# Linformer attention and a maxout layer on one core: first up blocks in two parts by heads, a split load, and a load moved

## The chip, the cores and the metric

The kernel runs on one core of a Trainium2 chip. The core has TensorE (matrix products; in profiles PE, its weight loads PEld), VectorE (DVE), ScalarE (ACT), GpSimd (POOL) and SyncE (SP), which here only issues transfers. Sixteen DMA engines move data between HBM and on-chip memory. The metric is the device time of one execution in microseconds, lower is better.

## What is computed

```python
k_proj = einsum('ks,bhsd->bhkd', E, k);  v_proj = einsum('ks,bhsd->bhkd', F, v)
attn = softmax(q @ k_proj^T / sqrt(64))           # over 64 projected keys
x = (attn @ v_proj) as rows (batch, position), columns (head, feature)
out = maximum(x @ w1, x @ w2) @ w_out
```

Batch 8, 8 heads, sequence 1024, head size 64, 64 projected keys; x is 8192 x 512, w1 and w2 are 512 x 1024, w_out is 1024 x 512. Inputs and output are float32.

## The kernel before

Loads go through GpSimd's queue and turn float32 into float16 on the way. The order of work on each engine is written out by hand: `manual_schedule` keeps the program's order, and each engine runs its own instructions in that order, with semaphores between the engines.

The maxout is rewritten: `max(h1, h2) = relu(x (w1 - w2)) + x w2`, so that `out = relu(x wd) w_out + x m`, with `wd = w1 - w2` (`step_wd`, L418, VectorE, 256 columns at a time) and `m = w2 w_out` (`step_w2t`, transposes L427 and a copy L433; `step_m`, L440 with the cast L444). An "up" is a product with wd and the relu, a "down" is the product with w_out and m together. Batch 0's ups are plain (`up_slots`: 8 blocks `fb` of 128 rows for each half `j` of the positions, each block a sum of four products L404 over r, the chunks of 128 columns of x; relu on ScalarE, L411, for the first three blocks and on VectorE, L413, for the others). Chunks r = 0, 1 are heads 0 to 3, chunks 2, 3 are heads 4 to 7. All later ups (`up_steps`, L558) and all downs (`down_steps`, L636) use a scheme with seven products instead of eight and sums on VectorE (L519 inputs, L475 weights, L573 and L660 outputs).

A batch's attention consists of: `step_kv` (L180, projections of k and v; casts L191, L193, L196), `step_kpt` (transposes of the projected k, L211, copy L216), `step_qt` (transposes of q, L237, copy L242), `step_sc` (scores, L266, exponential L306), `step_dn` (sums L278, logarithm L312), `step_inv` (exponential of minus the logarithm, L316), `step_at` (values L278, product with the inverse sums L329 into `xt`). Each of these works on a group (g: 4 heads, j: half the positions). From batch 2 on, q (L249), and from batch 3 on also the projected k (L223), are transposed by DMA transposes that SP issues, and `step_group` does scores (L266) of one group beside sums and values of the one before.

Batch 0's attention comes first and alone, with "warming" products `warm` (L140) where TensorE would wait. Then `slots`, the hand-made list: batch 0's up blocks, interleaved with step_wd and step_w2t, then the four step_m, then the units (a unit is half a batch; unit n's down pieces interleaved with unit n+1's ups). `steps` hangs further work behind named slots: `("P", n, p, i)` is piece i of product p of unit n's down, `("U", n, h, i)` an up product, `("G", n, h)` a mark for a group of scores. Batch 1's attention is hung behind step_m and the pieces of unit 0's down by the list of strings that begins `"kv", "", "kpt", "qt00 qt10"`.

On-chip memory for k, v and q has four buffers for all batches (`kvq`); the next load waits until one is free. `loads(b, ...)` issues a batch's loads. `step_gate` (L229) is a one-element copy on GpSimd that reads a transposed tile, so that loads behind it on that queue wait until the DMA transpose has landed. Accumulators lie in eight banks: four single ones (mm0 to mm3), which `mm_bank()` hands out in rotation, or by number, and two pairs (`att_banks`). After step_m the rotation is cut to mm2 and mm3, and downs use mm0 and mm1 by number.

```python
def mm_bank(dtype=FP32, n=None):
    if n is None:
        n = turn.pop(0)
        turn.append(n)
    return ps.tile([128, 512 if dtype == FP32 else 1024], dtype, tag=f"mm{n}", name="mm_ps")
```

Of the kernel before, what the change touches and what calls it, by code (L numbers as in the profile page):

```python
# [12 lines left out]
ALU = mybir.AluOpType  # L13
# [3 lines left out]
def kernel(  # L17
# [12 lines left out]
    nc = tc.nc  # L30
# [14 lines left out]
    const = ctx.enter_context(tc.tile_pool(name="const", bufs=1))  # L45
    kvq = ctx.enter_context(tc.tile_pool(name="kvq", bufs=4))
    proj = ctx.enter_context(tc.tile_pool(name="proj", bufs=2))
    soft = ctx.enter_context(tc.tile_pool(name="soft", bufs=3))
    qtp = ctx.enter_context(tc.tile_pool(name="qtp", bufs=2))
    stage = ctx.enter_context(tc.tile_pool(name="stage", bufs=4))  # L50
    xpool = ctx.enter_context(tc.tile_pool(name="xpool", bufs=3))
    gpool = ctx.enter_context(tc.tile_pool(name="gpool", bufs=2))
    opool = ctx.enter_context(tc.tile_pool(name="opool", bufs=4))
    ppool = ctx.enter_context(tc.tile_pool(name="ppool", bufs=4))
# [5 lines left out]
# [6 lines that stand above are left out]
    def att_banks(dtype=FP32):  # L66
        return ps.tile(
            [128, 2, 512 if dtype == FP32 else 1024], dtype, tag="att", bufs=2, name="att_ps"
        )
# [50 lines left out]
    w1_sb = big(1).rearrange("p (r f) -> p r f", r=NDC)  # L120
    w2_sb = big(2).rearrange("p (r f) -> p r f", r=NDC)
    wo_sb = const.tile([128, NFB, DM], FP16)
    for f0, f1 in ((0, 256), (256, 512), (512, DF)):
        for w_sb, w in ((w2_sb, moe_w2), (w1_sb, moe_w1)):
            for z in range(2):
                nc.gpsimd.dma_start(
                    out=w_sb.rearrange("p (g z) f -> p g z f", z=2)[:, :, z, f0:f1],
                    in_=w.rearrange("(g p z) f -> p g z f", p=128, z=2)[:, :, z, f0:f1],
                )
# [4 lines left out]
    junk = const.tile([1, 1], FP16)  # L134


    def warm(n):
        w_ps = mm_bank()
        for _ in range(n):
            nc.tensor.matmul(  # L140
                out=w_ps, lhsT=ones16[:, 0:128], rhs=ones16, start=True, stop=True
            )
# [29 lines left out]
    def step_kv(t, h0=0, h1=H, which="kv", att=False, dma=False):  # L172
        kv_ps = att_banks()[:, 0, :] if att else mm_bank()
        n = (h1 - h0) * D
        both = which == "v"
        for c in range(NC):
            for w in which:
                i = "kv".index(w)
                for r in range(2) if both else (i,):
                    nc.tensor.matmul(  # L180
                        out=kv_ps[r * KP : (r + 1) * KP, 0:n],
                        lhsT=eft[:, i, c, :],
                        rhs=t[w][:, h0:h1, c, :],
                        start=(c == 0), stop=(c == NC - 1),
                    )
        fl = lambda ap: ap[:, h0:h1].rearrange("p h z d -> p (h z d)")
        zd = lambda ap: ap.rearrange("p (h d z) -> p h z d", d=D // 2, z=2)
        if "k" in which:
            eng = nc.vector.tensor_copy if which == "k" else nc.scalar.copy
            kp = t["kp"][:, h0:h1]  # L190
            eng(out=kp[:, :, 0, :], in_=kv_ps[0:KP, 0:n].rearrange("p (h d) -> p h d", d=D))  # L191
        if both:
            nc.vector.tensor_copy(out=t["vp"][:, h0:h1], in_=zd(kv_ps[:, 0:n]))  # L193
        elif "v" in which:
            def finish_v():
                nc.vector.tensor_copy(out=t["vp"][KP:128, h0:h1], in_=zd(kv_ps[KP:128, 0:n]))  # L196
                if dma:
                    nc.vector.tensor_copy(out=kp[:, :, 1, :], in_=kp[:, :, 0, :])
                    step_kpt_dma(t)
                nc.vector.tensor_copy(out=fl(t["vp"][0:KP]), in_=fl(t["vp"][KP:128]))  # L200

            if att:
                return finish_v
            finish_v()
# [109 lines left out]
    def step_inv(t, g, j):  # L314
        ld = t["ld", g, j]
        nc.scalar.activation(out=ld, in_=ld, func=ACTF.Exp, scale=-1.0)  # L316

    def step_at(t, g, j, att=False):
        if "xt" not in t:
            new_xt(t)  # L320
        ld = t.pop(("ld", g, j))
        if att:
            both = att_banks()
            at_ps = [both[:, o, :] for o in range(2)]
        else:
            at_ps = [mm_bank() for _ in range(2)]
        values_into(t, g, j, at_ps)
        for o in range(2):
            nc.vector.tensor_tensor(  # L329
                out=x_out(t, g, j)[:, :, o, :],  # L330
                in0=at_ps[o].rearrange("q (z n) -> q z n", z=2),
                in1=ld[:, o, None, :].broadcast_to([128, 2, W]),
                op=ALU.mult,
            )
# [63 lines left out]
    def up_slots(t, j):  # L398
        t["gt", j] = gt = gpool.tile([128, NFB, HALF], FP16, tag="gt", name="gt_sb")
        for fb in range(NFB):  # L400
            def up(fb=fb):
                h_ps = mm_bank()
                for r in range(NDC):
                    nc.tensor.matmul(  # L404
                        out=h_ps,
                        lhsT=wd_sb[:, r, fb * 128 : (fb + 1) * 128],
                        rhs=t["xt"][:, r, :, j * W : (j + 1) * W],
                        start=(r == 0), stop=(r == NDC - 1),
                    )
                if fb < 3:  # L410
                    nc.scalar.activation(out=gt[:, fb, :], in_=h_ps, func=ACTF.Relu)  # L411
                else:
                    nc.vector.tensor_scalar_max(gt[:, fb, :], h_ps, 0.0)  # L413
            yield up


    def step_wd(f0):
        nc.vector.tensor_tensor(  # L418
            out=wd_sb[:, :, f0 : f0 + 256], in0=w1_sb[:, :, f0 : f0 + 256],
            in1=w2_sb[:, :, f0 : f0 + 256], op=ALU.subtract,  # L420
        )

    def step_w2t(f0):
# [309 lines left out]
    step_kpt(t, 4, 8)  # L733
    step_dn(t, 0, 1)
    step_inv(t, 0, 0)
    warm(4)
    step_qt(t, 4, 4, 0, NI // 2)
    step_qt(t, 4, 4, NI // 2, NI)
# [2 lines left out]
    step_sc(t, 1, 1)  # L741
    step_kv(t, 0, 4, "v")
    step_dn(t, 1, 0)
    step_inv(t, 1, 0)
    step_at(t, 0, 0)
    step_dn(t, 1, 1)
    step_inv(t, 0, 1)
    step_kv(t, 4, 8, "v")
    step_inv(t, 1, 1)
    step_at(t, 1, 0)  # L750
    step_wd(0)
    step_at(t, 0, 1, True)
    step_at(t, 1, 1, True)
    warm(4)


    load_all(tiles[1], 1, "k", k)
    u0, u1 = [*up_slots(t, 0)], [*up_slots(t, 1)]
    wt = [lambda f0=f0: step_w2t(f0) for f0 in range(0, DF, 256)]
    wd = [lambda f0=f0: step_wd(f0) for f0 in range(0, DF, 256)]  # L760
    f = lambda s, *a: lambda: s(tiles[0], *a)

    def loads(b, *names):
        for n in names:
            b_ = b + (n == "k" and b < 2)
            if b_ < B:
                load_all(tiles[b_], b_, n, {"k": k, "v": v, "q": q}[n])

    slots = [
        (0, u0[0]), (1, u0[1]), (None, lambda: loads(1, "v", "q", "k")), (2, u1[0]), (3, u1[1]),  # L770
        (None, wd[1]), (4, u0[2]), (None, wt[0]), (5, u0[3]),
        (None, wd[2]), (None, wt[1]), (6, u1[2]), (7, u1[3]), (8, u0[4]), (9, u0[5]), (None, wd[3]),
        (None, wt[2]), (10, u1[4]), (11, u1[5]), (12, u0[6]), (13, u0[7]), (None, wt[3]),
        (14, u1[6]), (15, u1[7]),
        *((16 + n, lambda n=n: step_m(n)) for n in range(NDC)),
    ]
# [26 lines left out]
    def at_slot(key, s, *a):  # L803
        steps.setdefault(key, []).append(lambda: s(*a))
# [12 lines left out]
    at_slot((0, 19), new_attn, t)  # L817
    at_slot((0, 19), lambda: turn.__setitem__(slice(None), [2, 3]))
    for n, x in enumerate((
        "kv", "", "kpt", "qt00 qt10", "", "sc00 sc10", "qt01", "qt11", "",  # L820
        "dn00 in00 dn10 in10", "", "", "at00 AT10 sc01", "", "",
    )):
        key = ("P", 0, (n - 1) // 2, (n - 1) % 2) if n else (0, 19)
        for name in x.split():
            if name[0] == "k":
                if name == "kpt":
                    at_slot(key, step_kpt, t, 0, H, True)
                else:
                    at_slot(key, step_kv, t, 0, H, "kv", True)
                    at_slot(key, loads, 2, "v", "q")  # L830
            else:
                g, j = int(name[2]), int(name[3])
                s_ = {"qt": step_qt, "sc": step_sc,
                      "dn": step_dn, "in": step_inv, "at": step_at, "AT": step_at}[name[:2]]
                args = (4 * g, 4, 2 * j, 2 * j + 2) if name[:2] == "qt" else (g, j)
                at_slot(key, s_, t, *args, *([True] if name[:2] == "AT" else []))
        if n in (1, 5):
            at_slot(key, step_t, 1, (0, 1) if n == 1 else (2, 3))
        if 6 <= n < 10:
            at_slot(key, sums_x, U[0, 1], ((2, 0, 1, 3)[n - 6],))  # L840
# [6 lines left out]
    at_slot(("G", 1, 0), step_qt_dma, t, 0, H // 2)  # L847
    at_slot(("G", 1, 0), step_qt_dma, t, H // 2, H)
    at_slot(("U", 1, 0, 6), step_gate, t, "qt")
    at_slot(("U", 1, 0, 6), loads, 3, "k", "v", "q")  # L850

    for b in range(3, B):
        t = tiles[b]
# [75 lines left out]
```

## Time and profile before

| | |
|---|---|
| median of 7 runs | 328.0 us (327.59 to 329.59) |
| the profiled execution's own time | 327.64 us |
| its span | 325.9 us |
| TensorE clock granted | full in all slices |
| loads issued by GpSimd (q0) | 28.31 MB, 54.7% of the 16 engines' span |
| stores, DMA transposes (q1) | 24.25 MB, 31.1% |
| k of batch 1, of batch 2 (1 MB each): issue to landing | 16.4 us, 29.0 us |

The span is the time from the first to the last instruction in the record. Columns of the timeline are start, duration, engine, line, operation, what it writes and reads, shape and count, then in brackets the idle time before it and what ended it. In a list of issues the last number is the time from issue to landing. In a table of windows the busy time and count of each engine stand in the order PE, PEld, DVE, ACT, POOL, then the TensorE clock, the DMA share and GB/s. Durations of products are given to the end of their pipeline; one behind another, a 128x512 product takes 0.216 us of TensorE.

### The profile page before, as it was taken

The numbers are of one execution on the slowest core, as the hardware profiler recorded it, in microseconds if no ns is written. First come the engines' busy times: TensorE is split into PE (matmuls) and PEld (weight loads), VectorE is DVE, ScalarE is ACT, GpSimd is POOL, SyncE is SP. The second block draws the span as 40 slices with busy tenths as digits, with TensorE's granted clock in tenths as the row PEclk, the third lists the DMA queues.
The fourth block names the chain that finished last, engine by engine and source line by source line (L and its number), as shares of the span: only waits on it lengthen the run. The fifth ranks groups of instructions, "written<-read, shape, count | busy, mean of one in ns | idle before, by whom it ended". The sixth has DMA issues, their size and how long they took to land.

```text
span 325.9 us, 9015 instructions
## 1 busy us (share of the span) xinstructions
PE 317.1 (97%) x3856; PEld 248.7 (76%) x3856; DVE 239.5 (74%) x424; ACT 201.1 (62%) x359; POOL 37.0 (11%) x56
## 2 busy tenths in 40 slices
PE   8989999999999999999999999999999999999994
PEld 4554547877887788878887888878887888888883
DVE  1355898985969788777967796977967796969572
ACT  2465322566776677667776777657776777765541
POOL 8646002003000200003000300003000000000000
PEclk9999999999999999999999999999999999999999
DMA  8999999987999799996999699989999120212032
GB/s 157 205 200 199 207 208 207 218 203 141 200 235 227 105 166 241 201 183 97 219 209 180 110 183 239 198 164 126 229 197 213 31 100 32 99 34 99 33 131 97
DMA packets 74680, 53.14 MB, mean 163 GB/s; under 512 B 29456, under 2 KB 74512, under 8 KB 74640
## 3 DMA queue, kind: packets, MB, share of 16 engines
q0 software_dynamic: 29376, 28.31, 54.7%
q1 hardware_dynamic: 45264, 24.25, 31.1%
q8 instruction: 30, 0.49, 0.6%
q14 instruction: 10, 0.08, 0.1%
HBM read 57.15 MB, written 16.78 MB: 227 GB/s over the span
## 4 chain that ended last, share of the span: by engine, by line
PE 87%; DMA 5%; DVE 3%; POOL 2%; issue 1%; ACT 0%; DVEq 0%; POOLq 0%
PE mm_ps L636 44%; PE mm_ps L558 26%; PE att_ps L180 4%; DMA v_sb<-in_v_dram 4%; PE mm_ps L404 4%; PE att_ps L278 3%; PE mm_ps L266 3%; PE mm_ps L440 2%; DMA big<-in_moe_w_dram 2%; POOL q_sb L102 1%; POOL k_sb L102 1%; DVE gt_sb L573 1%; DVE o_sb L660 1%; PE mm_ps L427 1%; PE mm_ps L237 0%
## 5 line engine op out<-in xcount | busy, mean ns | idle before, releaser
L529 ACT COPY p_sb<-mm_ps 128x512 f32<-128x512 f32 x172 | 97.1, 594 | 43.0 <-PE mm_ps L558 30.7
L636 PEld LDWEIGHTS <-big 128*128 128x128 f16 x768 | 73.6, 98 | 12.0 <-issue 3.5
L636 PE MATMUL mm_ps<-T_sb,big 128*128 128x256 f16 x576 | 77.9, 273 | 0.0
L573 DVE TENSOR_TENSOR gt_sb<-mm_ps,p_sb 128x512 f16<-128x512 f32 x56 | 38.5, 688 | 45.8 <-PE mm_ps L558 42.6
L558 PE MATMUL mm_ps<-big,big 128*128 128x256 f16 x336 | 50.4, 273 | 0.0
L558 PEld LDWEIGHTS <-big 128*128 128x128 f16 x448 | 43.8, 98 | 5.3 <-issue 0.2
L636 PEld LDWEIGHTS <-gt_sb 128*128 128x128 f16 x384 | 35.7, 98 | 9.7 <-issue 5.4
L636 PE MATMUL mm_ps<-wo_sb,gt_sb 128*128 128x256 f16 x256 | 42.9, 273 | 0.1
L558 PEld LDWEIGHTS <-wd_sb 128*128 128x128 f16 x336 | 32.9, 98 | 4.1 <-issue 0.4
L558 PE MATMUL mm_ps<-xt_sb,wd_sb 128*128 128x256 f16 x224 | 33.6, 273 | 0.2 <-ACT ex_sb L355 0.2
L355 ACT ACTIVATE ex_sb<-mm_ps 128x512 f16<-128x512 f32 x50 | 27.2, 597 | 9.6 <-PE att_ps L278 7.0
L381 DVE TENSOR_TENSOR xt_sb<-att_ps,ld_sb 128x1024 f16<-128x1024 f32 x26 | 31.7, 1219 | 0.1
L660 DVE TENSOR_TENSOR o_sb<-mm_ps,p_sb 128x512 f32<-128x512 f32 x32 | 21.9, 685 | 11.0 <-PE mm_ps L636 7.5
L636 PE MATMUL mm_ps<-m_sb,xt_sb 128*128 128x256 f16 x128 | 24.4, 273 | 0.0
L608 ACT ACTIVATE gt_sb<-mm_ps 128x512 f16<-128x512 f32 x28 | 16.8, 600 | 8.7 <-PE mm_ps L558 8.7
L519 DVE TENSOR_TENSOR big<-gt_sb 128x1024 f16<-128x1024 f16 x32 | 21.9, 685 | 0.2
L576 DVE TENSOR_SCALAR gt_sb<-gt_sb 128x512 f16<-128x512 f16 (+1 forms) x56 | 20.4, 363 | 1.9
L636 PE MATMUL mm_ps<-T_sb,gt_sb 128*128 128x256 f16 x128 | 21.5, 273 | 0.0
L636 PE MATMUL mm_ps<-wo_sb,big 128*128 128x256 f16 x128 | 21.5, 273 | 0.0
L636 PEld LDWEIGHTS <-xt_sb 128*128 128x128 f16 x192 | 18.8, 98 | 2.2
L229 POOL COPY junk<-kpt_sb 1x1 f16<-1x1 f16 x5 | 0.9, 177 | 162.5 <-DMA kpt_sb<-kp_sb 162.5
L573 DVE TENSOR_TENSOR gt_sb<-p_sb 128x512 f16<-128x512 f32 x28 | 19.1, 681 | 0.0
(85 smaller groups left out, 428.4 us busy)
## 6 DMA issues: line engine op xcount, KB each, us to landing
out_dram<-o_sb SPq DMA_DIRECT2D x63, 256.0 KB, 2.5
k_sb<-in_k_dram POOLq DMA_DIRECT2D x7, 1024.0 KB, 10.6
v_sb<-in_v_dram POOLq DMA_DIRECT2D x7, 1024.0 KB, 17.4
q_sb<-in_q_dram POOLq DMA_DIRECT2D x7, 1024.0 KB, 22.2
k_sb<-in_k_dram POOLq DMA_DIRECT2D x4, 256.0 KB, 6.2
q_sb<-in_q_dram POOLq DMA_DIRECT2D x4, 256.0 KB, 7.4
v_sb<-in_v_dram POOLq DMA_DIRECT2D x2, 512.0 KB, 12.1
big<-in_moe_w_dram POOLq DMA_DIRECT2D x8, 128.0 KB, 10.5
```

The source lines that it names most:

```text
L180: nc.tensor.matmul(out=kv_ps[r * KP : (r + 1) * KP, 0:n], lhsT=eft[:, i, c, :], rhs=t[w][:, h0:h1, c, :], start=(c == 0), stop=(c == NC - 1),)
L355: nc.scalar.activation(out=t["ex", g, j][:, e, :], in_=banks[e], func=ACTF.Exp, scale=scale)
L381: nc.vector.tensor_tensor(out=x_out(t, g, j).rearrange("q z o n -> q o z n"), in0=at_ps.rearrange("q o (z n) -> q o z n", z=2), in1=ld[:, ...
L404: nc.tensor.matmul(out=h_ps, lhsT=wd_sb[:, r, fb * 128 : (fb + 1) * 128], rhs=t["xt"][:, r, :, j * W : (j + 1) * W], start=(r == 0), stop= ...
L519: nc.vector.tensor_tensor(out=S(i), in0=x, in1=y, op=op)
L529: copy(out=x, in_=bank)
L558: nc.tensor.matmul(out=bank[:, m * W : (m + 1) * W], lhsT=w_[:, n_, (2 * d + m) * 128 : (2 * d + m + 1) * 128], rhs=a[:, n_, :], start=(n ...
L573: nc.vector.tensor_tensor(out=c_blk(j, c), in0=two(x), in1=two(y), op=ALU.add)
L576: nc.vector.tensor_scalar_max(ap, ap, 0.0)
L608: nc.scalar.activation(out=out, in_=in_, func=ACTF.Relu)
L636: nc.tensor.matmul(out=bank[:, i * CH : (i + 1) * CH], lhsT=a(c)[:, i * 128 : (i + 1) * 128], rhs=w_(c), start=(n is not None and m == (lo ...
L660: nc.vector.tensor_tensor(out=o_sb, in0=two(x), in1=two(y), op=ALU.add)
```

## The change

- `step_wd` takes a range of chunks r, and so does each up block. The first difference (columns 0 to 255) is made in two halves, and the first two blocks of each half of the positions are done in two parts: r = 0, 1 straight after batch 0's last `step_at`, r = 2, 3 in the slots. The loads of the first 256 columns of w1 and w2 are cut by halves g (r = 0, 1 and r = 2, 3) instead of by z (r = 0, 2 and r = 1, 3).
- In batch 0's attention, group (0, 1) is finished before group (1, 0); the second half of v's projection uses a pair bank and is cast on ScalarE; the last four warming products go. `soft` (inverse sums) gets four buffers, `xpool` (xt) two.
- w2t's third and fourth groups come ahead of u0[4].
- Batch 1's q comes in two loads, each with half of every partition's sequence rows. Batch 1's attention is hung one down piece later.
- Batch 3's k is loaded with batch 2's v and q, ahead of the gate that waits for batch 2's transposed q. Its v and q stay behind the gate.

```diff
@@ -45,10 +45,10 @@
     const = ctx.enter_context(tc.tile_pool(name="const", bufs=1))
     kvq = ctx.enter_context(tc.tile_pool(name="kvq", bufs=4))
     proj = ctx.enter_context(tc.tile_pool(name="proj", bufs=2))
-    soft = ctx.enter_context(tc.tile_pool(name="soft", bufs=3))
+    soft = ctx.enter_context(tc.tile_pool(name="soft", bufs=4))
     qtp = ctx.enter_context(tc.tile_pool(name="qtp", bufs=2))
     stage = ctx.enter_context(tc.tile_pool(name="stage", bufs=4))
-    xpool = ctx.enter_context(tc.tile_pool(name="xpool", bufs=3))
+    xpool = ctx.enter_context(tc.tile_pool(name="xpool", bufs=2))
     gpool = ctx.enter_context(tc.tile_pool(name="gpool", bufs=2))
     opool = ctx.enter_context(tc.tile_pool(name="opool", bufs=4))
     ppool = ctx.enter_context(tc.tile_pool(name="ppool", bufs=4))
@@ -120,7 +120,13 @@
     w1_sb = big(1).rearrange("p (r f) -> p r f", r=NDC)
     w2_sb = big(2).rearrange("p (r f) -> p r f", r=NDC)
     wo_sb = const.tile([128, NFB, DM], FP16)
-    for f0, f1 in ((0, 256), (256, 512), (512, DF)):
+    for g in range(2):
+        for w_sb, w in ((w2_sb, moe_w2), (w1_sb, moe_w1)):
+            nc.gpsimd.dma_start(
+                out=w_sb.rearrange("p (g z) f -> p g z f", z=2)[:, g, :, 0:256],
+                in_=w.rearrange("(g p z) f -> p g z f", p=128, z=2)[:, g, :, 0:256],
+            )
+    for f0, f1 in ((256, 512), (512, DF)):
         for w_sb, w in ((w2_sb, moe_w2), (w1_sb, moe_w1)):
             for z in range(2):
                 nc.gpsimd.dma_start(
@@ -134,8 +140,8 @@
     junk = const.tile([1, 1], FP16)
 
 
-    def warm(n):
-        w_ps = mm_bank()
+    def warm(n, att=False):
+        w_ps = att_banks()[:, 0, :] if att else mm_bank()
         for _ in range(n):
             nc.tensor.matmul(
                 out=w_ps, lhsT=ones16[:, 0:128], rhs=ones16, start=True, stop=True
@@ -190,7 +196,8 @@
             kp = t["kp"][:, h0:h1]
             eng(out=kp[:, :, 0, :], in_=kv_ps[0:KP, 0:n].rearrange("p (h d) -> p h d", d=D))
         if both:
-            nc.vector.tensor_copy(out=t["vp"][:, h0:h1], in_=zd(kv_ps[:, 0:n]))
+            eng = nc.scalar.copy if att else nc.vector.tensor_copy
+            eng(out=t["vp"][:, h0:h1], in_=zd(kv_ps[:, 0:n]))
         elif "v" in which:
             def finish_v():
                 nc.vector.tensor_copy(out=t["vp"][KP:128, h0:h1], in_=zd(kv_ps[KP:128, 0:n]))
@@ -398,15 +405,19 @@
     def up_slots(t, j):
         t["gt", j] = gt = gpool.tile([128, NFB, HALF], FP16, tag="gt", name="gt_sb")
         for fb in range(NFB):
-            def up(fb=fb):
-                h_ps = mm_bank()
-                for r in range(NDC):
+            def up(fb=fb, r0=0, r1=NDC):
+                if r0 == 0:
+                    t["up", j, fb] = mm_bank()
+                h_ps = t["up", j, fb]
+                for r in range(r0, r1):
                     nc.tensor.matmul(
                         out=h_ps,
                         lhsT=wd_sb[:, r, fb * 128 : (fb + 1) * 128],
                         rhs=t["xt"][:, r, :, j * W : (j + 1) * W],
                         start=(r == 0), stop=(r == NDC - 1),
                     )
+                if r1 < NDC:
+                    return
                 if fb < 3:
                     nc.scalar.activation(out=gt[:, fb, :], in_=h_ps, func=ACTF.Relu)
                 else:
@@ -414,10 +425,10 @@
             yield up
 
 
-    def step_wd(f0):
+    def step_wd(f0, r0=0, r1=NDC):
         nc.vector.tensor_tensor(
-            out=wd_sb[:, :, f0 : f0 + 256], in0=w1_sb[:, :, f0 : f0 + 256],
-            in1=w2_sb[:, :, f0 : f0 + 256], op=ALU.subtract,
+            out=wd_sb[:, r0:r1, f0 : f0 + 256], in0=w1_sb[:, r0:r1, f0 : f0 + 256],
+            in1=w2_sb[:, r0:r1, f0 : f0 + 256], op=ALU.subtract,
         )
 
     def step_w2t(f0):
@@ -733,6 +744,7 @@
     step_kpt(t, 4, 8)
     step_dn(t, 0, 1)
     step_inv(t, 0, 0)
+    step_inv(t, 0, 1)
     warm(4)
     step_qt(t, 4, 4, 0, NI // 2)
     step_qt(t, 4, 4, NI // 2, NI)
@@ -741,36 +753,46 @@
     step_sc(t, 1, 1)
     step_kv(t, 0, 4, "v")
     step_dn(t, 1, 0)
-    step_inv(t, 1, 0)
     step_at(t, 0, 0)
     step_dn(t, 1, 1)
-    step_inv(t, 0, 1)
-    step_kv(t, 4, 8, "v")
+    step_at(t, 0, 1)
+    step_inv(t, 1, 0)
+    step_kv(t, 4, 8, "v", True)
     step_inv(t, 1, 1)
-    step_at(t, 1, 0)
-    step_wd(0)
-    step_at(t, 0, 1, True)
+    step_wd(0, 0, 2)
+    step_at(t, 1, 0, True)
+    u0, u1 = [*up_slots(t, 0)], [*up_slots(t, 1)]
+    step_wd(0, 2, 4)
     step_at(t, 1, 1, True)
-    warm(4)
+    for u in u0, u1:
+        for x in u[0:2]:
+            x(r1=2)
 
 
     load_all(tiles[1], 1, "k", k)
-    u0, u1 = [*up_slots(t, 0)], [*up_slots(t, 1)]
     wt = [lambda f0=f0: step_w2t(f0) for f0 in range(0, DF, 256)]
     wd = [lambda f0=f0: step_wd(f0) for f0 in range(0, DF, 256)]
     f = lambda s, *a: lambda: s(tiles[0], *a)
 
     def loads(b, *names):
         for n in names:
-            b_ = b + (n == "k" and b < 2)
-            if b_ < B:
+            b_ = b + (n == "k" and b < 3)
+            if (b_, n) == (1, "q"):
+                alloc(tiles[1], "q")
+                for c in (0, NC // 2):
+                    nc.gpsimd.dma_start(
+                        out=tiles[1]["q"][:, :, c : c + NC // 2],
+                        in_=q[1].rearrange("h (p c) d -> p h c d", c=NC)[:, :, c : c + NC // 2],
+                    )
+            elif b_ < B:
                 load_all(tiles[b_], b_, n, {"k": k, "v": v, "q": q}[n])
 
     slots = [
-        (0, u0[0]), (1, u0[1]), (None, lambda: loads(1, "v", "q", "k")), (2, u1[0]), (3, u1[1]),
+        (0, lambda: u0[0](r0=2)), (1, lambda: u0[1](r0=2)), (None, lambda: loads(1, "v", "q", "k")),
+        (2, lambda: u1[0](r0=2)), (3, lambda: u1[1](r0=2)),
         (None, wd[1]), (4, u0[2]), (None, wt[0]), (5, u0[3]),
-        (None, wd[2]), (None, wt[1]), (6, u1[2]), (7, u1[3]), (8, u0[4]), (9, u0[5]), (None, wd[3]),
-        (None, wt[2]), (10, u1[4]), (11, u1[5]), (12, u0[6]), (13, u0[7]), (None, wt[3]),
+        (None, wd[2]), (None, wt[1]), (6, u1[2]), (7, u1[3]), (None, wt[2]), (None, wt[3]), (8, u0[4]), (9, u0[5]), (None, wd[3]),
+        (10, u1[4]), (11, u1[5]), (12, u0[6]), (13, u0[7]),
         (14, u1[6]), (15, u1[7]),
         *((16 + n, lambda n=n: step_m(n)) for n in range(NDC)),
     ]
@@ -817,8 +839,8 @@
     at_slot((0, 19), new_attn, t)
     at_slot((0, 19), lambda: turn.__setitem__(slice(None), [2, 3]))
     for n, x in enumerate((
-        "kv", "", "kpt", "qt00 qt10", "", "sc00 sc10", "qt01", "qt11", "",
-        "dn00 in00 dn10 in10", "", "", "at00 AT10 sc01", "", "",
+        "", "kv", "", "kpt", "qt00 qt10", "", "sc00 sc10", "qt01", "qt11", "",
+        "dn00 in00 dn10 in10", "", "", "at00 AT10 sc01", "",
     )):
         key = ("P", 0, (n - 1) // 2, (n - 1) % 2) if n else (0, 19)
         for name in x.split():
@@ -827,7 +849,7 @@
                     at_slot(key, step_kpt, t, 0, H, True)
                 else:
                     at_slot(key, step_kv, t, 0, H, "kv", True)
-                    at_slot(key, loads, 2, "v", "q")
+                    at_slot(key, loads, 2, "v", "q", "k")
             else:
                 g, j = int(name[2]), int(name[3])
                 s_ = {"qt": step_qt, "sc": step_sc,
@@ -847,7 +869,7 @@
     at_slot(("G", 1, 0), step_qt_dma, t, 0, H // 2)
     at_slot(("G", 1, 0), step_qt_dma, t, H // 2, H)
     at_slot(("U", 1, 0, 6), step_gate, t, "qt")
-    at_slot(("U", 1, 0, 6), loads, 3, "k", "v", "q")
+    at_slot(("U", 1, 0, 6), loads, 3, "v", "q")
 
     for b in range(3, B):
         t = tiles[b]
```

## The prediction

> **What bounds the kernel now.** I read the shares of the engines first, then stretches of time, then the timeline where TensorE was not full, and last the DMA view around the transfers that the change moves.
>
> ```profile
> PE 317.1 (97%) x3856; PEld 248.7 (76%) x3856; DVE 239.5 (74%) x424; ACT 201.1 (62%) x359; POOL 37.0 (11%) x56
> ...
> 80.10:325.00 244.90, 241.28 (x2964) 201.87 (x2961) 186.33 (x329) 164.68 (x304) 11.41 (x17) 1.00 0.78 153
> ```
>
> TensorE is the bound. From 80 us on it is busy 241.3 of 244.9 us, and no part of the diff alters what is computed there. So the change is worth what it alters in TensorE's clock up to about 80 us. The stretch around the first up blocks:
>
> ```profile
> 23.66 1.04 PE L140 MATMUL mm_ps<-ones 128*128 128x512 f16 x4
> 25.38 4.71 PE L404 MATMUL mm_ps<-xt_sb,wd_sb 128*128 128x512 f16 x20 [0.68 <-DVE wd_sb L418]
> 25.24 2.48 DVE L329 TENSOR_TENSOR xt_sb<-att_ps,ld_sb 128x512 f16<-128x512 f32 x4
> 32.37 0.69 DVE L418 TENSOR_TENSOR wd_sb<-big,big 128x1024 f16<-128x1024 f16 x1 [0.24 <-DMA big<-in_moe_w_dram]
> 41.21 7.07 PE L440 MATMUL mm_ps<-wo_sb,big 128*128 128x512 f16 x32
> 48.32 0.59 ACT L444 CAST m_sb<-mm_ps 128x512 f16<-128x512 f32 x1 [1.14 <-PE mm_ps L440]
> ```
>
> The four warming products fill a wait, the up blocks start at 25.38, and their second half waits for VectorE's last product with the inverse sums (25.24 + 2.48 = 27.72). The third wd difference (32.37) waits for weights. Then the second attention stage, where the moved transfers are:
>
> ```profile
> q_sb<-in_q_dram POOLq DMA_DIRECT2D x1, 1024.0 KB, 18.6
> ...
> 69.96 4.23 SPq L249 DMA_TRANSPOSE qt_sb<-q_sb  x2
> ...
> qt_sb<-q_sb SPq DMA_TRANSPOSE x1, 4.5
> ...
> 76.79 0.40 PE L266 MATMUL mm_ps<-qt_sb,kpt_sb 64*32 64x256 f16 x16
> ...
> 76.85 0.18 POOL L229 COPY junk<-qt_sb 1x1 f16<-1x1 f16 x1 [24.67 <-DMA qt_sb<-q_sb]
> 77.36 0.88 POOL L102 DMA_DIRECT2D k_sb<-in_k_dram  x1 [0.34 <-PE mm_ps L266]
> ```
>
> Batch 2's q, issued at 51.29, lands 18.6 us later, at 69.9. Only then can SP issue the two DMA transposes. The first (heads 0 to 3) lands at 69.96 + 4.5 = 74.4, and batch 2's first scores, which read it, run at 76.79: 2.3 us of slack. Batch 3's k is issued at 77.36, behind the gate. So in the present kernel nothing else is in the load queue while the transposes run.
>
> **What the Trainium skill says.** "DMA: Bandwidth & Descriptors", section "Issuing engines are not separate DMA queues": transfers of all issuers interleave on the same 16 DMA engines. The same page, "Queues, rings and completion order": each engine goes round its queues packet by packet. The trace agrees: in the 2.5 us from 59.5 loads and a store moved 0.34 and 0.26 MB side by side.
>
> ```profile
> q0 software_dynamic: 718, 0.73, 124.7%
> out_dram<-o_sb SPq DMA_DIRECT2D x1, 256.0 KB, 6.2
> ...
> q0 software_dynamic: 338, 0.34, 79.5%
> q1 hardware_dynamic: 272, 0.26, 38.4%
> ```
>
> The first two lines are the window 56 to 59.5. The store issued at 56.06 moved nothing in it: its first packet came 3.5 us after the issue, because loads were queued. The transposes of 69.96 found the load queue empty, and their first packet came at 71.24, 1.3 us after the issue. "PSUM — Partial Sum Buffer", section "Terms", says that TensorE must not write a bank while another engine reads it. This is the wait I count below for the last m cast.
>
> **The change, part by part.**
>
> *VectorE's order at the start.* Unchanged until 21.01, where the first xt product starts. Products of this form follow each other each 0.605 us (2.48 less 0.07, over 4). After: four of them (heads 0 to 3) to 23.43; half a wd difference, 128x512, 0.42 (as the rows of that form); two products to 25.0; the other half; two products, done at 26.64. Before it was 27.72. What went is the second vp cast (0.42, now ScalarE's, at 22.40, where it has nothing due) and a wait of 0.61; what came is 0.15, since two halves cost 0.84 and the whole 0.68. ScalarE's Ln of the fourth group no longer waits for a buffer (it waited 0.91), as soft has four. The weights needed land in time: those of the first half at 22.6, of the second at 24.0, and the order of the bytes is about the same.
>
> *TensorE's first blocks.* The first halves can start at 23.43 + 0.42 + 0.06 = 23.91: 8 products at 0.216 to 25.64, four more to 26.50, then it waits for 26.64 + 0.06, and four more end at 27.57. Before, these 16 ended at 29.07 (25.38 + 4.71, less the fill of 0.16 and the fifth block's 0.86). Gain so far 1.5. The warming products that go lay in a wait and are worth nothing themselves.
>
> *Next wall, the weights.* u0[4] needs the third wd difference, at 33.06 in both kernels (its last transfer lands at 32.25). Before, it started at 33.41 with two transpose groups (w2t, 0.45 each) still to do. After, with those two put ahead of it, TensorE arrives at 32.80 and starts at 33.12. The gain is cut to 33.41 + 0.90 - 33.12 = 1.2.
>
> *Next wall, a bank.* The warming call took a PSUM bank of the rotation; in its place the calls change so that the last m block (step_m 3) lies in bank 0. The first down piece, now straight behind it, writes bank 0. Before, it lay in bank 2 and batch 1's kv (1.85) stood between. So TensorE waits for the cast: 48.32 + 0.59 against the end of issue at 48.13 is 0.78, with the wake-up 0.85. Gain left 0.35.
>
> *A piece later.* kv then comes at 48.5, after v of batch 1 (47.46). q in two loads: half the run per packet. The weights' loads with such packets moved about 193 GB/s against 206, so 1 MB takes 0.3 longer, and all behind it lands 0.3 later. The first half lands near 50.1, the transposes of q come at 52.9, so the present wait for q (0.1 at 52.55) goes. VectorE's qt copies come one piece later relative to the products, and the wait before the second score group (0.35) shrinks to some 0.15. Gain at 76 us: about 0.6. xt with two buffers costs nothing: batch 2's xt is first written in unit 2, after the last read of batch 0's in unit 1.
>
> *Batch 3's k ahead of the gate.* It needs batch 1's q buffer, free when the last q transposes end (58 us), and so lies in the load queue right behind batch 2's q. That q lands near 70.3 (0.3 from the split, and some more store packets ahead of it). k then moves until 75.4 or later, exactly while the transposes should. They are issued at 70.4. Their start is bounded below by 1.3 us after (no load ahead) and is 3.6 after by the store's case: 74.0. Moving 0.5 MB at the trace's 210 GB/s takes 2.5, and the landing follows 0.6 behind the last packet: 77.1 if they then have the engines to themselves, 78.4 if what is left of k (0.27 MB, 1.3 us) goes first. I take 77.8. TensorE would be at these scores at 76.2. It waits to 77.9 against 76.79 before: **1.1 us later than before**. Queued behind on TensorE is all that follows, and later stages have no waits to absorb it. The second half of qt, needed at 84.8, lands near 81, so it costs nothing. The gate opens some 4 us later, but k has landed, and v and q of batch 3 come ahead of their present 95.7 and 101.1.
>
> *Sum.* Against the profiled execution: span 325.9 + 1.1 = 327.0, with the 1.7 around it 328.7. That execution (327.64) lies 0.4 under the median of the runs, 328.0; on the median it is **329.1**.
>
> **Rivals.**
>
> *A, the transposes aren't held up* (not slower). Place: the first transpose of batch 2. Price: the 1.1 above. Decided by whether it lands by 76.2. For it: they come from another queue, and from 66.3 to 70 stores moved 0.73 MB against 0.19 of loads. Against: the 3.5 us before a store's first packet. Then the 0.6 stays: 327.4.
>
> *B, the start gives more.* If the weights land some tenths earlier, or the bank wait is covered, up to 1.5 survives at 76 us, with A's landing: 326.5. For it: VectorE's time is well founded. Against: both walls are plain in the rows.
>
> *C, k goes first altogether* and the transposes' small packets (256 B against 1024) take turns one to one with k's: the landing slips to 79.0 or more, and the issues on SP, which are 1.9 and 2.3 us each, stretch. Then 2.4 later: 330.4.
>
> **How the numbers follow.** Main case 0.47, A 0.22, B 0.16, C 0.15. What a measurement here can tell from no change is 0.3%, 1.0 us. The main case runs from +0.4 to +1.7 (328.4 to 329.7), about two thirds of it slower by more than that: 0.30, with C 0.45. Same: 0.17 of the main case and 0.18 of A, 0.35. Faster: B and the edge of A, 0.20. The range takes A whole and most of B and C: 326.9 to 330.4.
>
> **What would show it.** Right: up blocks from 23.9; the third wd difference still near 32.4; TensorE waiting 0.8 for ScalarE before the first down piece; the first qt transpose landing after 77 and TensorE idle for it before batch 2's first scores. Wrong: load packets absent from 70 to 75, or the first transpose landing by 76; then the time is A's or B's. A TensorE wait after 80 us that is not there now would break the step that says all else is unchanged.

## The result: three microseconds later

| | before | after |
|---|---|---|
| median of the runs | 328.98 us (31 runs) | 331.99 us (12 runs) |
| profiled execution: its own time, its span | 327.64, 325.9 | 331.74, 330.0 |
| up blocks of batch 0 start | 25.38 | 24.57 |
| batch 2's q landed | 69.88 | 73.50 |
| its first DMA transpose landed | 74.44 | 80.87 |
| batch 2's first scores start | 76.79 | 80.92 |

The ratio is 1.0100, with a 95% interval of 1.0081 to 1.0119: the kernel became 3.0 us slower. First the shares of the engines after:

```profile
PE 316.6 (96%) x3852; PEld 248.3 (75%) x3852; DVE 238.2 (72%) x424; ACT 201.0 (61%) x360; POOL 38.0 (12%) x57
```

And of the same profile a window from soon after batch 2's first scores on (busy time and count of PE, PEld, DVE, ACT and POOL, then clock, DMA share, GB/s):

```profile
84.20:329.10 244.90, 241.31 (x2964) 201.94 (x2961) 186.27 (x329) 164.88 (x304) 13.05 (x19) 1.00 0.75 149
```

As many microseconds as in the stretch shown of before, as many products (2964), and TensorE busy as long. So in this profile nothing was lost after batch 2's first scores. They start 4.13 us later, and the span is 4.1 us longer. The timeline up to there:

```profile
24.57 4.82 PE L413 MATMUL mm_ps<-xt_sb,wd_sb 128*128 128x512 f16 x20 [0.33 <-DVE wd_sb L429]
...
34.07 0.69 DVE L429 TENSOR_TENSOR wd_sb<-big,big 128x1024 f16<-128x1024 f16 x1 [2.64 <-DMA big<-in_moe_w_dram]
...
34.82 2.55 PE L413 MATMUL mm_ps<-xt_sb,wd_sb 128*128 128x512 f16 x11 [1.06 <-DVE wd_sb L429]
...
48.85 0.59 ACT L455 CAST m_sb<-mm_ps 128x512 f16<-128x512 f32 x1 [1.14 <-PE mm_ps L451]
...
49.48 0.60 PE L647 MATMUL mm_ps<-wo_sb,gt_sb 128*128 128x256 f16 x4 [0.67 <-ACT m_sb L455]
...
53.31 0.88 POOL L102 DMA_DIRECT2D q_sb<-in_q_dram  x1
60.13 0.88 POOL L102 DMA_DIRECT2D k_sb<-in_k_dram  x1 [5.94 <-PE mm_ps L244]
...
73.58 7.64 SPq L256 DMA_TRANSPOSE qt_sb<-q_sb  x2
...
77.54 0.40 PE L285 MATMUL att_ps<-ex_sb,vp_sb 64*32 64x256 f16 x16
80.92 0.41 PE L273 MATMUL mm_ps<-qt_sb,kpt_sb 64*32 64x256 f16 x16 [2.98 <-DMA qt_sb<-q_sb]
```

Read it from the bottom. TensorE reached batch 2's first scores after the products that start at 77.54, and stood 2.98 us until the transposed q was there. SP needed 7.64 us to issue the two transposes (4.23 before). Above it are the two waits that use up the gain of the start: 1.06 for the third wd difference, whose weights landed at 33.95, and 0.67 for the bank that the last m cast (48.85 + 0.59) still read. The chain of waits passes through the same place:

```profile
73.52 0.06 PE mm_ps L647
73.58 7.29 DMA qt_sb<-q_sb
80.87 0.04 issue
80.92 0.46 PE mm_ps L273 x16
```

Batch 3's k, issued at 60.13 and landed at 79.08, moves while the transposes should. The DMA view in three stretches, 73.6 to 76, 76 to 79.1 and 79.1 to 80.9 (packets, MB, share of the engines; q0 the loads, q1 here the transposes and, up to 74.8, the end of stores):

```profile
DMA packets 534, 0.51 MB, mean 213 GB/s; under 512 B 42, under 2 KB 534, under 8 KB 534
...
q0 software_dynamic: 470, 0.48, 119.5%
q1 hardware_dynamic: 64, 0.03, 5.7%
...
DMA packets 1044, 0.41 MB, mean 132 GB/s; under 512 B 856, under 2 KB 1044, under 8 KB 1044
...
q1 hardware_dynamic: 841, 0.22, 93.3%
q0 software_dynamic: 203, 0.19, 37.6%
...
DMA packets 1924, 0.48 MB, mean 269 GB/s; under 512 B 1924, under 2 KB 1924, under 8 KB 1924
```

First k moves almost alone, at 213 GB/s in all. While both move, everything together reaches 132 GB/s: 841 small packets and 203 large ones take 3.1 us. Only when k has landed do the transposes run, at 269 GB/s. So while they share the engines both are slow.

### The profile page after: what moved, and what is told of

The parts are those of the page before. It is cut to its first block, busy times and chain, and to the rows that moved or that the text cites. A ratio compares the mean times of both kernels' runs of the same rounds, so it can differ in the third digit from the quotient of the medians.

```text
span 330.0 us, 9009 instructions
## 1 busy us (share of the span) xinstructions
PE 316.6 (96%) x3852; PEld 248.3 (75%) x3852; DVE 238.2 (72%) x424; ACT 201.0 (61%) x360; POOL 38.0 (12%) x57
## 4 chain that ended last, share of the span: by engine, by line
PE 83%; DMA 9%; POOL 3%; DVE 2%; issue 1%; ACT 1%; DVEq 0%; POOLq 0%
PE mm_ps L647 43%; PE mm_ps L569 25%; DMA v_sb<-in_v_dram 4%; PE att_ps L186 4%; PE att_ps L285 3%; PE mm_ps L273 3%; DMA big<-in_moe_w_dram 3%; DMA qt_sb<-q_sb 2%; PE mm_ps L413 2%; PE mm_ps L451 2%; POOL q_sb L102 1%; POOL big L132 1%; POOL k_sb L102 1%; DVE gt_sb L584 1%; DVE o_sb L671 1%
## 5 line engine op out<-in xcount | busy, mean ns | idle before, releaser
L647 PEld LDWEIGHTS <-big 128*128 128x128 f16 x768 | 73.6, 98 | 12.0 <-issue 3.5
L647 PE MATMUL mm_ps<-T_sb,big 128*128 128x256 f16 x576 | 77.8, 273 | 0.0
L362 ACT ACTIVATE ex_sb<-mm_ps 128x512 f16<-128x512 f32 x50 | 27.2, 597 | 12.7 <-PE att_ps L285 7.0
```

Source lines behind the costliest of these rows:

```text
L362: nc.scalar.activation(out=t["ex", g, j][:, e, :], in_=banks[e], func=ACTF.Exp, scale=scale)
L647: nc.tensor.matmul(out=bank[:, i * CH : (i + 1) * CH], lhsT=a(c)[:, i * 128 : (i + 1) * 128], rhs=w_(c), start=(n is not None and m == (lo ...
```

## The experiments

Two theories stood against each other: the whole loss is batch 3's k beside the first transposes (so k alone brings it, and without k it goes); or the weights' loads, cut by g instead of by z, start the lateness (last weights landed at 33.95 against 32.25). Ratios are to runs of the kernel before on the same chip, each with its 95% interval, as they stand on record; they are not the quotients of the two medians.

### k behind the gate again, k alone, half of k

The changed kernel with k back behind the gate:

```diff
-            b_ = b + (n == "k" and b < 3)
+            b_ = b + (n == "k" and b < 2)
-                    at_slot(key, loads, 2, "v", "q", "k")
+                    at_slot(key, loads, 2, "v", "q")
-    at_slot(("U", 1, 0, 6), loads, 3, "v", "q")
+    at_slot(("U", 1, 0, 6), loads, 3, "k", "v", "q")
```

> The changed kernel with batch 3's k back behind the gate. Theory: k's packets beside the two DMA transposes are what makes TensorE wait 3.1 us before batch 2's first scores. Then the first transpose lands 4.5 us after batch 2's q as before (not 7.4), the wait is under 0.5 us, and the time falls by about 3 us from the changed kernel, to within 1 us of the kernel before on either side. Rival: batch 2's q itself lands too late (73.5 us in the changed kernel against 69.9), so the wait stays above 1.5 us whatever is behind it in the queue, and the time stays over 1 us above the kernel before.

Measured: 328.97 against 329.03 us, ratio 0.9993 (0.9975 to 1.0011). The loss is gone. SP's and TensorE's timeline:

```profile
71.02 4.17 SPq L256 DMA_TRANSPOSE qt_sb<-q_sb  x2
...
77.33 0.40 PE L273 MATMUL mm_ps<-qt_sb,kpt_sb 64*32 64x256 f16 x16
```

The issues are short again and the scores have no bracket, so no wait. But there is no gain either, and in this profile none reached the scores at all: they start 0.5 us later than the 76.79 of before. The up blocks began late here, at 25.59, though batch 0's v landed early, at 21.49. TensorE's clock had been at half from 7.8 to 11.2 us, as the windows 5 to 10 and 10 to 15 show (0.78 and 0.88):

```profile
5.00:10.00 5.00, 4.51 (x25) 2.86 (x26) 0.76 (x2) 0.59 (x1) 4.14 (x6) 0.78 1.22 210
10.00:15.00 5.00, 4.84 (x69) 2.41 (x67) 2.00 (x4) 0.84 (x1) 2.83 (x4) 0.88 1.24 204
```

So this profile cannot tell where the gain of the start goes in the other executions.

The kernel before with nothing but k ahead of the gate (the same three edits the other way round):

> The kernel before with batch 3's k ahead of the gate as the only edit. Theory: the first transpose lands 7.4 us after batch 2's q (69.9), at 77.3, where the scores were at 76.8, so TensorE waits some 0.6 us and the kernel is slower by 0.3 to 1.5 us. Its first issue on SP takes over 4 us where it took 1.9. If k alone costs the whole loss (rival), slower by 3 us. If transposes were not disturbed by it, no change.

Measured: 332.06 against 329.03, ratio 1.0078 (1.0055 to 1.0102).

```profile
80.53 0.41 PE L266 MATMUL mm_ps<-qt_sb,kpt_sb 64*32 64x256 f16 x16 [1.91 <-DMA qt_sb<-q_sb]
```

k alone brings the loss, against an expectation of 0.3 to 1.5 us: its rival, the whole loss, came true. Here q landed at 72.21 and the first transpose 8.3 us later. The changed kernel with half of it ahead, heads 0 to 3:

```diff
+    def half_k(i):
+        if i == 0:
+            alloc(tiles[3], "k")
+        load(tiles[3], "k", k, 3, i * H // 2, (i + 1) * H // 2)
-                    at_slot(key, loads, 2, "v", "q", "k")
+                    at_slot(key, loads, 2, "v", "q")
+                    at_slot(key, half_k, 0)
+    at_slot(("U", 1, 0, 6), half_k, 1)
```

> The changed kernel with only heads 0 to 3 of batch 3's k (half the bytes) ahead of the gate, the rest behind it. In three runs the first transpose landed 1.7 us after the k load beside it, not at a share of the engines. If the transposes in effect wait until the loads beside them are through, half of k is through some 2.8 us after batch 2's q, the first transpose lands about 4.5 us after q as undisturbed (at most 5.5), and the time is that of the kernel with all of k behind the gate, within 0.5 us. If they are slowed in proportion to the bytes beside them, it lands 6 us after q or later and half of the 3 us loss stays.

Measured: ratio 0.9993 (0.9977 to 1.0008), and no wait at the scores in the profile. The half landed at 75.82 and the first transpose at 77.75, 5.5 us after q (4.5 without k beside it, 7.4 with the whole of it), just when TensorE came. So the loss is not in proportion to the bytes: half of them delay the transpose by about a third as much, and cost nothing that is seen.

### The weights' loads

The changed kernel with the old cut by z, and the kernel before with the new cut by g (the same edit the other way round):

```diff
-    for g in range(2):
-        for w_sb, w in ((w2_sb, moe_w2), (w1_sb, moe_w1)):
...
-    for f0, f1 in ((256, 512), (512, DF)):
+    for f0, f1 in ((0, 256), (256, 512), (512, DF)):
```

> The changed kernel with the first weights loaded as before (by z), all else kept. If the new cut of the weights slows the load stream, the last weights land near 32.3 us again (33.95 in the changed kernel), batch 2's q some 1.7 us earlier, and the time falls by about 1.7 us. If the late stream comes from something else (the split q and its place in the queue, or chance), no change within 0.5 us.

> The kernel before with the first weights loaded in the new cut as the only edit. If that cut slows the stream, the third wd difference starts near 34.1 us instead of 32.4, TensorE waits over 1 us there, and the kernel is slower by 1 to 1.5 us. If not, no change within 0.5 us, and the last weights land near 32.3 us.

Measured: 1.0094 (1.0070 to 1.0118) and 1.0006 (0.9989 to 1.0022). The cut does nothing that the times show. The last weights landed at 31.95 by z and at 33.65 by g in these two profiles, but at 32.24 by g in the run with k behind and at 33.38 by z in the run with k alone: the lateness of the load stream, 1.7 us between these four, differs from run to run with either cut.

### Where the gain of the start stays

k behind, and the first up blocks moved off bank 0 by turning the rotation, so that the last m block doesn't lie in the bank of the first down piece:

```diff
     step_at(t, 1, 1, True)
+    turn[:] = turn[2:] + turn[:2]
     for u in u0, u1:
```

> The changed kernel with batch 3's k behind the gate and the bank rotation turned by two, so that the last m block lies in bank 2 again. Theory: the 0.84 us wait for the last m cast before the first down piece goes and TensorE keeps it to the end, as nothing waits at batch 2's scores: 0.5 to 0.9 us less than with k behind the gate alone, so some 0.2 to 0.3% below the kernel before. Rival: the next wait takes it (v of batch 1 for kv, or q for its transposes), and the time stays that of the kernel before.

Measured: ratio 1.0002 (0.9984 to 1.0021). The bank wait is gone from the profile, and in it the first transpose, whose q landed late, at 72.75, is waited for:

```profile
77.32 0.41 PE L273 MATMUL mm_ps<-qt_sb,kpt_sb 64*32 64x256 f16 x16 [0.46 <-DMA qt_sb<-q_sb]
```

The same bank edit with k left ahead:

> The changed kernel, k still ahead of the gate, with the bank rotation turned by two. Theory: TensorE comes 0.84 us earlier to batch 2's scores and waits there 0.84 us longer, since the landing of the first transpose sets the end: time within 0.4 us of the changed kernel's 332.0. Rival: if TensorE's own clock set the end, 0.84 us less.

Measured: 332.12 us, ratio 1.0108 (1.0073 to 1.0143): the time of the changed kernel, as expected. TensorE came 1.3 us earlier than in the profile of the changed kernel. It did not wait the 0.84 us longer that were expected but only 0.1, since q and with it the transpose landed 1.2 us earlier too:

```profile
76.20 0.40 PE L285 MATMUL att_ps<-ex_sb,vp_sb 64*32 64x256 f16 x16
79.68 0.63 PE L273 MATMUL mm_ps<-qt_sb,kpt_sb 64*32 64x256 f16 x16 [3.08 <-DMA qt_sb<-q_sb]
```

k behind and the bank edit, with batch 1's q in one load again:

> As the run before, with batch 1's q in one load. If the split is needed, TensorE waits at the transposes of q for the whole of it (about 0.5 us more than with the split) and the time rises by that. If it only costs load rate, all later loads land 0.3 us earlier and the time is the same or up to 0.3 us lower.

Measured: 328.60, ratio 0.9991 (0.9974 to 1.0007). Not told apart from no change. In this profile the up blocks started at 27.23, and the scores, without a wait, at 78.15. From 10 to 15 us TensorE did 37 products where the changed kernel did 80:

```profile
10.00:15.00 5.00, 5.00 (x37) 2.88 (x36) 1.16 (x3) 0.00 (x0) 2.84 (x4) 1.00 1.24 204
```

The clock's record begins only at 14.2 us in this profile (at 4.7 in the changed kernel's), so the 1.00 says nothing of the time before.

If the first transposes hold the gain back in most executions, batch 2's q must land earlier. On top of k behind and the bank edit, batch 2's loads were ordered so:

```diff
+    def q_by_heads(t, b):
+        alloc(t, "q")
+        load(t, "q", q, b, 0, H // 2)
+        load_all(t, b, "v", v)
+        load(t, "q", q, b, H // 2, H)
-                    at_slot(key, loads, 2, "v", "q")
+                    at_slot(key, q_by_heads, tiles[2], 2)
```

> Batch 3's k behind the gate, the first up blocks' m3 bank taken from the free pair, and batch 2's loads in the order q of heads 0 to 3, v, q of heads 4 to 7. Theory (the start's gain is real, and only the landing of batch 2's q with its transposes takes it back): the first transpose lands before 73 us, batch 2's first scores wait for nothing, and 0.6 to 1.4 us of the gain show, 327.6 to 328.4 beside 328.9 before. Rival (the transposes starve until the loads beside them are through, or a later wait takes the gain): the wait is there again or comes later, 328.6 to 329.2.

Measured: 328.0 against 329.0, ratio 0.9965 (0.9947 to 0.9983). This version beats both kernels, by 1.0 us (0.6 to 1.7) the one before.

```profile
24.18 4.61 PE L413 MATMUL mm_ps<-xt_sb,wd_sb 128*128 128x512 f16 x20 [0.60 <-DVE wd_sb L429]
...
64.04 9.61 SPq L256 DMA_TRANSPOSE qt_sb<-q_sb  x2
...
75.45 0.40 PE L273 MATMUL mm_ps<-qt_sb,kpt_sb 64*32 64x256 f16 x16
```

The scores start at 75.45 without a wait, against 76.79. The expected landing before 73 was missed: issued at 64.04, the first transpose landed at 73.77, only 2.1 us after the last of the loads beside it (71.67). It got little done in nearly 8 us beside the loads, and yet it was early enough. The loads are not the whole reason: three stores had been issued on SP just before it,

```profile
61.28 2.65 SPq L662 DMA_DIRECT2D out_dram<-o_sb  x3
...
DMA packets 1339, 1.33 MB, mean 247 GB/s; under 512 B 54, under 2 KB 1338, under 8 KB 1338
```

and from 64 to 69.4 (the second line) 0.71 MB of loads and 0.60 on SP's queue moved, with only 54 packets under 512 bytes; the transpose's have 256. So its late start is that of the stores ahead of it too, and the two were not taken apart.

The kernel before with this order of loads alone:

> The kernel before with one edit: batch 2's loads in the order q of heads 0 to 3, v, q of heads 4 to 7. It tells where the gain of the run with this order on top of the change's start came from (328.0 beside 329.0 before). Theory (the gain came from the start, the up blocks by heads and the free bank; the kernel before does not wait for its first transposes at all, so it has nothing to win there): the same time as before within 0.4 us, 328.6 to 329.4. Rival (the order of batch 2's loads is itself worth the gain, by earlier transposes): 327.8 to 328.3.

Measured: 328.81 against 329.01, ratio 0.9993 (0.9978 to 1.0008). Alone the order is worth nothing that is seen: it frees a gain that the start makes. And the version with q by heads on top of the change's start, with half of k ahead too:

> The same with heads 0 to 3 of batch 3's k ahead of the gate and the rest behind it. Theory (what counts is only when the loads beside the first transposes are through): the first transpose is early enough, so no wait at batch 2's first scores, and the same time as with all of the k behind within 0.3 us. Rival (the half k holds the first transposes up): a wait of 0.5 to 2 us at these scores, and as much more time.

Measured: 328.9 against 329.0, ratio 0.9997 (0.9979 to 1.0015): the gain is lost again, 0.9 us more than with all of k behind on the same chip, and the expected equality was missed. The wait that the rival puts this down to is not in the profile, but that was the fastest of the 14 executions (327.49), and TensorE came late in it, at 76.68, after up blocks that started at 25.51. Its first transpose landed at 76.13; against the 75.45 of the best version TensorE would have waited 0.7 us. So the cause is likely the rival's, but not shown.

### The clock after the wait

In the profiles of k alone, of the old cut and of the bank edit with k ahead, TensorE's clock halves around the end of the wait (from 0.4 us before it to 1.6 after). k alone, in four windows (columns as before: busy times, then clock, DMA share, GB/s):

```profile
76.00:80.50 4.50, 2.62 (x44) 1.93 (x42) 1.94 (x4) 1.09 (x2) 0.00 (x0) 1.00 1.31 178
80.50:82.10 1.60, 1.40 (x25) 0.94 (x26) 0.00 (x0) 1.09 (x3) 0.00 (x0) 0.99 1.93 230
82.10:85.50 3.40, 3.40 (x18) 2.43 (x16) 1.35 (x3) 1.98 (x4) 1.09 (x3) 0.50 0.23 75
85.50:90.00 4.50, 4.50 (x50) 3.86 (x50) 4.41 (x8) 2.84 (x5) 0.84 (x1) 1.00 0.92 115
```

From 82.10 to 85.50 the clock is 0.50, and TensorE works on 18 products. The first fifty from the scores on take 6.07 us in place of 4.59, 1.5 us more. In the profile of the changed kernel it does not happen, but in most of its timed runs the mean clock is lower: 0.995 or less in 9 of 12. Over all kernels with the whole k ahead it is 30 of 35 runs, over the eight others tried 23 of 136. One such dip of 3.4 us at half clock in 330 makes a mean of 0.995. The mean doesn't say where the dip lies: the profile of the bank edit with k ahead has a second one, from 7.6 to 11.1 us, and the one with k behind has its only one there. Among the changed kernel's runs, three with 0.997 or more average 331.2 us, seven with 0.993 or 0.994 average 332.1, two with 0.989 average 333.6. So the first dip goes with some 0.9 us, an estimate from few runs.

"TensorE: Matmul & The Clock Gate" in the Trainium skill, section "Why this matters for your kernels", says to leave no idle gaps of over about 3 us between bursts, since a window of idle brings the clock back to half; its section "What's actually happening" gives the window as 3413 ns, free-running. The 3.4 us at 0.50 agree, and so does the rest of this profile's clock: full for 75.09 us from 6.98 on, half for 3.41, full for 245.76, which is 22 and 72 times 3.41. The gap is not quite as stated: 1.91 us of wait went with the dip here, and 2.98 us in the changed kernel's profile did not. To take the idle away, ten warming products were put ahead of the scores of the changed kernel:

```diff
+            if t is tiles[2] and (g, j) == (0, 0):
+                fill(10)
```

> The changed kernel with ten warming products put on TensorE just ahead of batch 2's first scores; nothing else moves. Theory (part of the loss is the TensorE clock, which drops to half for 3.4 us after the idle of 2 to 3 us in front of these scores): the idle is shortened, the clock stays at full, the fifty matmuls after the scores take about 4.6 us again instead of up to 6.0, and the median falls by 0.5 to 1.5 us, to 330.5 to 331.5, while the wait for the first transpose itself stays. Rival (the clock plays no part in the median; the loss is the transposes' delay alone): within 0.3 us of the changed kernel, about 332.

Measured: 333.61, ratio 1.0150 (1.0120 to 1.0180), slower still, and the mean clock was again 0.995 or less in four of five runs.

```profile
82.40 0.41 PE L273 MATMUL mm_ps<-qt_sb,kpt_sb 64*32 64x256 f16 x16 [1.52 <-DMA qt_sb<-q_sb]
```

And the window from 85 on:

```profile
85.00:88.40 3.40, 3.40 (x22) 2.51 (x21) 2.53 (x4) 1.53 (x3) 1.75 (x2) 0.63 0.37 32
```

The filling ended with 1.52 us still to wait, since the first transpose came 3.1 us after k here, and the clock fell all the same (0.63 over this stretch, whose last 0.9 us are at full clock again). Neither theory foresaw that. That the wait brings the dip rests on the count of runs and the place of the dips. That filling it all would keep the clock up was not shown, and why this kernel is slower than the changed one stays open.

## Why the prediction was off

*The start.* The up blocks were to start at 23.9; they did at 24.57 with batch 0's v landed 0.8 us later than before (22.04 against 21.25), and at 24.18 in the best version, whose v landed at 21.38. The halves of wd took 0.41 and 0.42 as counted. Right, but only where TensorE's clock is full early: where it fell or came late in the first 15 us, the blocks started at 25.5 to 27.2 (four profiles, with v landed at 21.1 to 21.8), no earlier than before.

*The two walls.* The wait for the weights was put at 0.32 and was 1.22, start to start, because the weights landed 1.7 later in that run. The bank wait was put at 0.85 and was 0.84. Right in kind, and the bank to 0.01.

*What is left at 76 us.* TensorE was to come to these scores at 76.2. In the profile of the changed kernel it came at 77.8, as the weights were late. But in the run with the old cut, whose weights landed at 31.95 and so as early as in the profile of before, it came at 76.1 (the scores follow these products by 0.22 us where nothing is waited for):

```profile
75.89 0.40 PE L279 MATMUL att_ps<-ex_sb,vp_sb 64*32 64x256 f16 x16
```

So the 0.6 was right for a load stream as early as the one it was worked out from. With k behind the gate the time is that of before all the same (ratio 0.9993); with the bank wait away and the transposes early 1.0 us came out. What the sum missed is that such a gain is easily lost again: at the start, to the clock or to late weights, and at the end to the first transposes, which in the kernel before landed only 2.3 us ahead of the scores. This slack wanders with the load stream, and in the profile with k behind and the bank edit it was already below zero.

*k beside the transposes, the step that failed.* The mechanism and the place were those of the main case; the landing of the first transpose, put at 77.8, and with it the price of 1.1 us, was mis-sized. It landed at 80.87. Term by term:

| term | foreseen | measured, changed kernel |
|---|---|---|
| q landed | 70.3 | 73.50 |
| from the issue to the transpose's first packets | 3.6 us | 2.1 us (73.58 to 75.6) |
| k still to move then | 0.27 MB, 1.3 us | 0.27 MB, 3.4 us (75.6 to 79.08) |
| from these packets to the landing | 3.8 us (3.1 to 4.4) | 5.2 us |

The amount of k left is that of the sum, as the loads' line for 75.6 to 79.1 shows:

```profile
q0 software_dynamic: 280, 0.27, 46.7%
```

The sum moved k and the transposes one after the other at 210 GB/s, so that sharing would cost nothing but k's own 1.3 us. Together they moved at 132. That from q's landing to the transpose's it was 7.4 us, where 7.5 had been foreseen, is luck: the start was 1.5 us shorter and the shared stretch 1.4 us longer. In the other profiles with the whole k ahead the start took 3.0 to 3.5 us and the stretch 4.3 to 5.8, and most of the delays were longer:

| whole k ahead, in | q landed | k landed | first transpose landed | after k | after q | wait, us |
|---|---|---|---|---|---|---|
| the change | 73.50 | 79.08 | 80.87 | 1.8 | 7.4 | 2.98 |
| k alone | 72.21 | 78.80 | 80.49 | 1.7 | 8.3 | 1.91 |
| weights by z | 70.65 | 77.10 | 78.79 | 1.7 | 8.1 | 2.5 |
| bank edit | 72.23 | 77.83 | 79.64 | 1.8 | 7.4 | 3.08 |
| warming products | 73.10 | 79.23 | 82.35 | 3.1 | 9.3 | 1.52 after 2.3 of filling |

Rival C came nearest: SP's two issues stretched from 4.23 to 7.64 us, and the landing went past 79. But the packets did not take turns one to one (841 to 203), 0.22 MB of the transposes moved while k did, and C's 2.4 us fell short too.

The larger miss in this one profile is q itself, 3.2 us late, while TensorE came 1.6 later than the 76.2 foreseen: its wait was 3.2, start to start, in place of 1.7. Why q was so late stays open. In the profiles with the split q it landed between 70.65 and 73.50, in those without between 69.88 and 72.21 (the order by heads left aside), and the prediction was built on the earliest of them all.

*What the medians add up to.* Foreseen +1.1, measured +3.0. The 0.6 gained at the start is no part of the gap: as long as TensorE waits for the transpose, its own arrival doesn't count. Of the 1.9 between, about 0.8 goes with the clock, which no step had (an estimate: 331.99 less the 331.2 of the three runs without a dip). The delay after q, 8.1 us on average over the table's five profiles and 7.8 without the last, is 0.3 to 0.6 more than foreseen. The remaining 0.5 to 0.8, worked out as a difference, would be the landing of q; single profiles scatter too much to show it.

*After 80 us* nothing changed in this profile, as said: 241.31 us busy against 241.28. Where the clock fell around the wait, the products after it took up to 1.5 us more. The second transpose, put near 81, landed at 82.67 and made no wait.

## What to carry to other kernels

A load moved ahead of a gate must be asked what it travels beside: here a DMA transpose with loads beside it landed 1.7 to 2.1 us after the last of them in seven profiles (3.1 and 4.1 in two others), so in this kernel a load may be moved up only if it is through some 2 us, better 4, before the transposed data is wanted. A gain made early shows only if the next landing is early too: when an edit brings nothing, look for the transfer that now ends last, and move its load before giving the edit up. Look at the clock before explaining a start that is late or early in one profile. And an idle of 2 to 3 us on TensorE may cost more than its length: around such waits the clock dropped in most profiles here.

## What the runs showed of the hardware

- Loads of 1024-byte packets and transposes of 256-byte packets side by side moved 132 GB/s together; k with hardly any beside it 213, the transposes alone 269 in the changed kernel and 201 in the kernel before (71.2 to 73.8 us).
- The issue of a DMA transpose on SP takes longer when loads are queued: the first 1.88 us before, 4.62 in the changed kernel, and 7.65 in the best version, where it was issued 7.6 us before the loads were through, with three stores ahead of it.
- A first transpose with no load beside it landed 4.5 to 4.6 us after q in five profiles of kernels with k behind the gate; issued 7.6 us before the loads beside it were through, and behind stores, it landed 9.7 us after its issue.
- TensorE's clock went to 0.50 for 3.4 us around waits of 1.5 to 3.1 us in four profiles, and not around one of 2.98 us. In two profiles it did so from about 7.7 us on, in the start, and in two more its record began only at 10.9 and 14.2 us; in these four the up blocks started 1.3 to 3.1 us later than the 24.18 of the best version.
